# Storing two heads' gK and gV with one DMA of 16 KiB rows in the second pass of an attention backward kernel

## The chip, the cores and the metric

The kernel runs on one core of one Trainium2 chip. The metric is device time in microseconds (us), lower is better: 890.82 us is the median of 3 runs of the kernel before (889.17 to 891.23). A core has five engines with instruction streams of their own: PE (TensorE, matmul), DVE (VectorE), ACT (ScalarE), POOL (GpSimd) and SP (SyncE, which here only issues DMAs). An engine takes its instructions in order; an instruction that waits holds up all behind it. 16 DMA engines move data between HBM and the on-chip memory of 128 partitions.

## The reference

Forward and backward of one decode step: layer norm, attention against a cache, and an MLP, each with a residual, for B=2 sequences, H=32 heads, 4096 cached positions, head size 128, model width 640. What the change touches is the gradient of the cache:

```python
q = (ln(x) @ wq)                        # [2, 32, 1, 128]
p = softmax(q @ k.T * Dh**-0.5)         # k, v: [2, 32, 4096, 128]
h = x + (p @ v) @ wo
h2 = h + relu(ln(h) @ w1) @ w2
# outputs: h2, gx, gK (out_2), gV (out_3), gwq, gwo, gw1, gw2
```

With go the gradient of a head's attention output, gV of a head is the outer product of p and go, and gK is the outer product of gs = p * (v @ go - dot) and the scaled q. Each is 4096 x 128 in bf16, 1 MiB, and there are 64 heads (32 for each sequence).

## The kernel before, in words

**Tiles.** One head's K, V, gK or gV is a tile of 128 partitions x 32 rows x 128 columns: partition p holds cache rows 32p to 32p+31, so a transfer of one tile moves one contiguous row of 8 KiB for each partition (`natural`, L500). 13 such tiles ("homes", `NBIG`) lie in the pool `big`; more come from `big1` (2, where the first pass's pool `pkp` was), from `big2` (1) and from the six tiles of wo when they are no longer needed. `take`, `give` and `share` pass homes between four uses: ld (loads), g (gradients to be stored), f (weight gradients to be stored, called ot) and q (wq and MLP weights).

**Two passes.** The first pass (`p1_iter`, iteration i) loads K and V of each of the 64 heads and makes scores, softmax and the attention output. The second pass (`p2_iter`, iteration j, in the order of the list `turns`) loads V again as Wt, but for 6 kept heads of each sequence, and makes gV and gK. From i=40 on, every second iteration of the first pass has one of the second pass mixed in. When the first pass ends, j=14 to 63 are left: **the second pass alone**, the subject here. Beside it run in small steps (`bg_step`) the MLP's backward, `go_group` (32 reductions at L711 over wo, one for each head of the second sequence), `fin_gen` (weight gradients: PE at L1093, an ACT copy at L1099, a store issued by POOL at L1101) and `gx_gen` (wq loaded once more, 40 reductions at L711).

**One head of the second pass** (`p2_iter`): four groups of four PE transposes of Wt (t_ps, L482), each copied out of PSUM by ACT (t_sb, L487) and multiplied with go by PE (dp, L495); two matmuls that broadcast go and q to all partitions (L985), scaled by ACT into rb (L990); p doubled by POOL (pp, L992); one DVE instruction for gs (L965). Then `outer_half` (L954) makes half of a gradient tile in one DVE instruction: 2 for gK of the head before, 2 for gV of this head. Up to j=32 ACT makes 8 of the 32 row blocks of gV (L1024). SP stores each tile: gK at L1004, gV at L1025. The load of a later head is issued by `pump` as soon as a home is free in the order of the program; it waits on SP for the last transposes of the tile that it overwrites. All of SP's DMAs go through one queue in the order of the program.

**Buffers of this stage before:** ld=10 (6 of them hold kept V, 4 are ahead), g=5; from j=37 on ld=4, g=7 and three tiles of wo, f=3, q=2 and three tiles of wo; once the background is done, still more for g.

Of the kernel before, what the change touches and what calls it, by code (L numbers as in the profile page):

```python
# [7 lines left out]
FP32 = mybir.dt.float32  # L8
BF16 = mybir.dt.bfloat16
ALU = mybir.AluOpType  # L10
# [5 lines left out]
def kernel(  # L16
# [89 lines left out]
    owned = dict(free)  # L106
    wanted = {}
    pools = [big] * NBIG
    home_of = {}
    given_at = {}  # L110

    def take(tag, shape, name):
        assert free[tag] > 0, (tag, name)
        free[tag] -= 1
        k = homes[tag].pop(0)
        t = pools[k].tile(shape, BF16, tag=tag_of.get(k, f"big{k}"), bufs=1, name=name)
        home_of[id(t)] = (tag, k, t)
        return t

    def goes_to(tag):  # L120

        if owned[tag] > wanted.get(tag, len(pools)):
            for other in homes:
                if owned[other] < wanted.get(other, 0):
                    return other
        return tag

    def give(t, to=None):
        tag, k, _ = home_of.pop(id(t))
        to = to or goes_to(tag)  # L130
        owned[tag] -= 1
        owned[to] += 1
        free[to] += 1
        homes[to].append(k)
        given_at[k] = step[0]
# [14 lines left out]
                    d[tag] -= 1  # L150
                    d[to] += 1

    tag_of = {}

    def more_home(tag, pool, name=None):
        if name:
            tag_of[len(pools)] = name
        homes[tag].append(len(pools))
        pools.append(pool)
        free[tag] += 1  # L160
        owned[tag] += 1
# [70 lines left out]
    NPS = 52  # L232
    P_bf = cols.tile([128, NPS, NSC], BF16)
    P_free = list(range(NPS))
    P_slot = {}
    ga = cols.tile([128, B, NF], FP32)
    nc.vector.memset(ga[:], 0.0)
# [127 lines left out]
    qc = pkp.tile([128, H, B], BF16)  # L365
    WH = 6
    NWO = -(-H // WH)
    wo_t = [wop.tile([128, NSC * 128], BF16, tag=f"wo{t}", bufs=1, name="wo_t") for t in range(NWO)]

    def wo_of(h, c0, c1):  # L370
        return wo_t[h // WH][:, (h % WH) * D + c0:(h % WH) * D + c1]
# [73 lines left out]
    pairs = [(b, h) for b in range(B) for h in range(H)]  # L445
    NP1 = len(pairs)
    KEPT = (6, 6)
    GROUPS = []
    for b in range(B):
        first = H - KEPT[b]  # L450
# [497 lines left out]
    def pairs_view(t):  # L948
        return t.rearrange("p s (a two) -> p s a two", two=2)

    def outer_half(dst, row, colp, k, short=0):
        n = HALF - short
        sl = slice(k * HALF, k * HALF + n)
        nc.vector.tensor_tensor(  # L954
            out=pairs_view(dst[:, sl, :]),
            in0=row.rearrange("p (a two) -> p a two", two=2)[:, None, :, :].to_broadcast([128, n, 64, 2]),
            in1=colp[:, sl, None, :].to_broadcast([128, n, 64, 2]), op=ALU.mult)
# [10 lines left out]
        P_free.append(P_slot.pop((bp, hp)))  # L968
        return gsp

    def p2_iter(j, busy, act=0, store=None):
        store = store or nc.gpsimd

        c = S2[j] if j < NP1 else None
        p = S2.get(j - 1)
        if p is not None:
            bp, hp = turns[j - 1]
            gsp = p2_gs(j - 1)
        if c is not None:
            b, h = turns[j]  # L980
            go = gom[:, h, b, :, :]

            bank = pst([128, 512], FP32, "sps", "dp_ps")
            for k, col in enumerate((goc, qsc)):
                nc.tensor.matmul(bank[:, 128 + k * 128:256 + k * 128],  # L985
                                 lhsT=col[:, h, b:b + 1].to_broadcast([128, 128]), rhs=ident_bf[:],
                                 start=True, stop=True)
            c["dp"] = bank[:, 0:NSC]
            rb = mats.tile([128, 256], BF16, tag="rb", bufs=3, name="rb")
            nc.scalar.activation(out=rb[:], in_=bank[:, 128:384], func=ACT.Copy, scale=rt[:, b, h:h + 1])  # L990
            pp = small.tile([128, NSC, 2], BF16, tag="pp", bufs=2, name="pp")
            nc.gpsimd.tensor_copy(out=pp[:], in_=P_bf[:, P_slot[(b, h)], :, None].to_broadcast([128, NSC, 2]))  # L992
            c.update(rb=rb, pp=pp)
            if act:
                pa = small.tile([128, act], FP32, tag="pa", bufs=2, name="pa")
                nc.gpsimd.tensor_copy(out=pa[:], in_=P_bf[:, P_slot[(b, h)], NSC - act:NSC])
            c["T0"] = pair_transpose(c["W"], 0, busy=busy)
        if p is not None:
            gK = take("g", [128, NSC, 128], "gK")
            outer_half(gK, p["rb"][:, 128:256], gsp, 0)  # L1000
        yield
        if p is not None:
            outer_half(gK, p["rb"][:, 128:256], gsp, 1)
            store.dma_start(out=natural(out_2, bp, hp), in_=gK[:])  # L1004
            give(gK)
            del S2[j - 1]
        yield
        if c is None:
            return
        c["T1"] = pair_transpose(c["W"], 1, busy=busy)  # L1010
        pair_matvec(c["dp"], c.pop("T0"), 0, go)
        yield
        c["T2"] = pair_transpose(c["W"], 2, busy=busy)
        pair_matvec(c["dp"], c.pop("T1"), 1, go)
        yield
        c["T3"] = pair_transpose(c["W"], 3, busy=busy)
        give(c["W"], "g" if j < H and j != 1 and owned["g"] < 3 else None)
        pair_matvec(c["dp"], c.pop("T2"), 2, go)
        gV = take("g", [128, NSC, 128], "gV")
        outer_half(gV, c["rb"][:, 0:128], c["pp"], 0)  # L1020
        yield
        outer_half(gV, c["rb"][:, 0:128], c["pp"], 1, act)
        for k in range(act):
            nc.scalar.activation(out=gV[:, NSC - act + k, :], in_=c["rb"][:, 0:128], func=ACT.Copy, scale=pa[:, k:k + 1])  # L1024
        store.dma_start(out=natural(out_3, b, h), in_=gV[:])  # L1025
        give(gV)
        yield


    def p2_tail(j):  # L1030

        p = S2[j]
        bp, hp = turns[j]
        gsp = p2_gs(j)
        yield
        gK = take("g", [128, NSC, 128], "gK")
        outer_half(gK, p["rb"][:, 128:256], gsp, 0)
        yield
        outer_half(gK, p["rb"][:, 128:256], gsp, 1)
        nc.gpsimd.dma_start(out=natural(out_2, bp, hp), in_=gK[:])  # L1040
        give(gK)
        del S2[j]
        yield
# [254 lines left out]
    def p2_step():  # L1298
        nonlocal g2
        try:  # L1300
            next(g2)
        except StopIteration:
            g2 = None

    for n, (i, j) in enumerate(plan):
        all_go = all(("go", B - 1, h) in done for h in range(H))
        if i is None and plan[n - 1][0] is not None:
            pkp.release()
            big1 = tc.alloc_tile_pool(name="big1", bufs=1)
            for _ in range(2):  # L1310
                more_home("ld", big1)
            share(ld=KEPT[1] + 4, g=5)
        if ("w1", B - 1) in done:
            for t in range(NWO):
                if t not in late and all(("go", B - 1, h) in done for h in range(t * WH, min(H, (t + 1) * WH))) and \
                        (t < NWO - 1 or all_go):
                    late[t] = ("g", "g", "g", "q", "q", "q")[len(late)]
                    more_home(late[t], wop, f"wo{t}")
        lq, ll, lg = [sum(v == tag for v in late.values()) for tag in ("q", "ld", "g")]
        if fin is not None and not bg2 and not bg3:  # L1320
            share(ld=4, g=12 + 6 * (lq > 0))
        elif fin is not None and j >= H + KEPT[1] - 1:
            share(ld=4 + ll, g=7 + lg, f=3, q=2 + lq)
        if j is not None:
            while g2 is not None:
                p2_step()
            if j < NP1:
                bg_until(("go", *turns[j]))
            if i is not None and n + 1 < len(plan) and plan[n + 1][1] is None:
                g2 = p2_whole(j)  # L1330
            else:
                g2 = p2_iter(j, 0, 8 if i is None and j <= H else 0, nc.sync if i is None else None)
        if i is None and ("w1", 1) in done and fin is None:
            wts.release()
            fin = tc.alloc_tile_pool(name="fin", bufs=1)
            big2 = tc.alloc_tile_pool(name="big2", bufs=1)
            more_home("f", big2)
            banks.update(sps=[2, 3], o=[4, 5, 6])
            bg2.append(("fin", fin_gen(fin)))
            bg3.append(("gx", gx_gen(fin)))  # L1340
        if i == 12:
# [9 lines left out]
        if i is None:  # L1351
            mixed[0] = False
            spread[0] = 2
            at_k[0] = 1
            k = 0
            while g2 is not None:
                p2_step()
                pump()
                slot[0] = int(k in ((1, 3, 5) if j <= H else (1, 4)))
                k += 1  # L1360
                bg_step(0, rate)
                bg_step(1, RATE2 * (0.4 if spreading[0] else 1.0))
                bg_step(2, RATE3)
            continue
# [64 lines left out]
```

## Time and profile before

| | |
|---|---|
| median of 3 runs | 890.82 us |
| the profiled execution | 887.9 us |
| its span, first to last instruction | 886.1 us (1.8 us lie around it) |
| PE, DVE, ACT, POOL busy | 736.0, 690.8, 478.0, 155.8 us |
| moved by DMA | 361.87 MB, mean 408 GB/s |
| SP's queue | 317.04 MB in 49096 packets |
| first store that SP issues (gK of head 13, the stage alone begins) | issued at 466.7 us |
| last gK store (head 63) | issued at 866.1 us |

A span is cut into windows in the views by stage; for each, the busy time of every engine, the clock granted to PE (1 is full), the share of time in which the 16 DMA engines had packets, and GB/s. A DMA share of 1.01 means that packets overlap by a little and no engine is without one. "Landing" is the time from an issue to the last of the 16 engines' completion marks.

### The profile page before, as it was taken

What the parts mean: (1) busy time and instruction counts of PE and PEld (TensorE: products, weight loads), DVE (VectorE), ACT (ScalarE), POOL (GpSimd) and SP (SyncE); (2) the same over time, 40 slices, a digit from 0 to 9 for tenths busy, and PEclk for the clock granted to TensorE, in tenths of its full rate; (3) what the DMA queues carried; (4) which work ended last, traced back from release to release, by engine and by line L of the source; (5) the groups of instructions that cost most, each with busy time, mean ns of one, the idle gap of its engine ahead of it and who ended that gap; (6) DMA issues with size and microseconds to landing.
All of it is one profiled execution on the core that took longest, in us unless ns stands there. A gap on an engine that the chain in (4) does not pass through costs nothing.

```text
span 886.1 us, 24945 instructions
## 1 busy us (share of the span) xinstructions
PE 736.0 (83%) x10215; PEld 614.3 (69%) x10215; DVE 690.8 (78%) x1309; ACT 478.0 (54%) x1241; POOL 155.8 (18%) x264
## 2 busy tenths in 40 slices
PE   4999899999999998878967777878878896937971
PEld 4888788888888887777856666656757665625640
DVE  2666698877888887777868797678989998799750
ACT  1344343344565655455546777767756555526661
POOL 1344344343210000010011110011010001101200
PEclk9999899999999999999996556555666756556565
DMA  9999999999889999999999999999999999999995
GB/s 377 425 417 417 421 413 420 424 423 416 323 298 392 424 424 426 423 424 426 423 405 415 422 425 425 425 422 412 419 425 414 419 419 427 415 426 421 408 425 229
DMA packets 56115, 361.87 MB, mean 408 GB/s; under 512 B 5712, under 2 KB 11728, under 8 KB 15296
## 3 DMA queue, kind: packets, MB, share of 16 engines
q1 hardware_dynamic: 49096, 317.04, 86.5%
q0 software_dynamic: 6864, 43.22, 11.7%
q8 instruction: 80, 1.31, 0.5%
q14 instruction: 35, 0.29, 0.1%
q10 hardware_dynamic: 40, 0.01, 0.0%
HBM read 211.11 MB, written 149.13 MB: 407 GB/s over the span
## 4 chain that ended last, share of the span: by engine, by line
PE 38%; DMA 21%; DVE 19%; issue 12%; ACT 8%; SPq 0%; POOL 0%; ACTq 0%; POOLq 0%; DVEq 0%
PE t_ps L482 17%; DMA Vt<-in_A_v_cache_dram 10%; PE m_ps L516 9%; DVE gK L954 5%; DVE gV L954 5%; DMA out_dram<-gK 4%; DVE rows L711 4%; DVE pk L523 3%; ACT t_sb L487 3%; PE s_ps L495 3%; PE u_ps L545 3%; DMA out_dram<-ot 2%; ACT gV L1024 2%; DMA wqs<-in_A_wq_dram 2%; PE dp_ps L495 2%
## 5 line engine op out<-in xcount | busy, mean ns | idle before, releaser
L487 ACT COPY t_sb<-t_ps 128x512 f32<-128x512 f32 x479 | 274.2, 587 | 208.7 <-PE t_ps L482 205.4
L495 PEld LDWEIGHTS <-t_sb 128*128 128x128 bf16 x4096 | 177.7, 102 | 57.2 <-ACT t_sb L487 28.8
L482 PE MATMUL t_ps<-ident_f,Wt 128*128 128x128 f32 x832 | 192.6, 381 | 9.0 <-DMA Wt<-in_A_v_cache_dram 8.4
L523 DVE TENSOR_TENSOR pk<-Kt,ep 128x2048 bf16<-128x2048 bf16 x128 | 156.3, 1222 | 39.7 <-ACT ep L570 31.4
L516 PE MATMUL m_ps<-pk,Vt 128*128 128x129 bf16 x2048 | 170.6, 222 | 13.5 <-DMA Vt<-in_A_v_cache_dram 13.5
L482 PEld LDWEIGHTS t_ps<-ident_f,Wt 128*128 128x128 f32 x832 | 134.7, 197 | 38.1 <-issue 30.6
L482 PE MATMUL t_ps<-ident_f,Kt 128*128 128x128 f32 x1024 | 157.0, 286 | 4.1 <-DMA Kt<-in_A_k_cache_dram 3.4
L954 DVE TENSOR_TENSOR gK<-rb,gsp 128x2048 bf16<-128x2048 bf16 x128 | 153.2, 1222 | 8.9 <-DMA out_dram<-gV 7.1
L516 PEld LDWEIGHTS <-Vt 128*128 128x128 bf16 x2048 | 124.5, 98 | 43.5 <-issue 27.7
L954 DVE TENSOR_TENSOR gV<-rb,pp 128x2048 bf16<-128x2048 bf16 (+1 forms) x128 | 143.3, 1140 | 2.7 <-DMA out_dram<-gK 2.6
L482 PEld LDWEIGHTS t_ps<-ident_f,Kt 128*128 128x128 f32 x1024 | 113.5, 145 | 7.8 <-ACT t_sb L487 3.8
L533 POOL COPY pk<-ep 128x16 bf16<-128x16 bf16 x78 | 83.2, 1069 | 155.6 <-ACT ep L570 80.5
L495 PE MATMUL dp_ps<-gom,t_sb 128*128 128x2 bf16 x2048 | 95.3, 168 | 16.9 <-ACT t_sb L487 16.0
L495 PE MATMUL s_ps<-qm,t_sb 128*128 128x2 bf16 x2048 | 87.6, 164 | 1.3 <-DVE t_sb L485 1.3
L1099 ACT CAST ot<-o_ps 128x512 bf16<-128x512 f32 (+3 forms) x152 | 66.8, 493 | 5.1 <-DMA out_dram<-ot 3.0
L992 POOL COPY pp<-P_bf 128x64 bf16<-128x64 bf16 x64 | 30.3, 478 | 163.6 <-DVE gV L954 152.0
L630 ACT CAST wo_t<-m_ps 128x128 bf16<-128x128 f32 x55 | 14.6, 266 | 78.1 <-PE m_ps L516 77.9
L711 DVE CUSTOM_DVE_ANT_0 rows<-wqs,gqr 128x1024 bf16<-128x1024 bf16 x40 | 48.9, 1221 | 9.6 <-DMA wqs<-in_A_wq_dram 9.4
L990 ACT ACTIVATE rb<-dp_ps,rt 128x256 bf16<-128x256 f32 x64 | 30.3, 473 | 44.2 <-PE dp_ps L985 43.3
L711 DVE CUSTOM_DVE_ANT_0 rows<-wo_t,rows 128x640 bf16<-128x640 bf16 x64 | 52.4, 819 | 0.8 <-ACT rows L688 0.4
L1024 ACT ACTIVATE gV<-rb,pa 128x128 bf16<-128x128 bf16 x152 | 46.5, 392 | 6.4 <-DMA out_dram<-gV 6.4
L711 DVE CUSTOM_DVE_ANT_0 rows<-w_t,rows 128x640 bf16<-128x640 bf16 (+2 forms) x53 | 42.3, 799 | 2.9 <-ACT rows L688 2.7
(205 smaller groups left out, 690.3 us busy)
## 6 DMA issues: line engine op xcount, KB each, us to landing
Kt<-in_A_k_cache_dram SPq DMA_DIRECT2D x64, 1024.0 KB, 18.7
Vt<-in_A_v_cache_dram SPq DMA_DIRECT2D x64, 1024.0 KB, 15.1
Wt<-in_A_v_cache_dram SPq DMA_DIRECT2D x52, 1024.0 KB, 16.4
out_dram<-gK SPq DMA_DIRECT2D x51, 1024.0 KB, 16.7
out_dram<-gV SPq DMA_DIRECT2D x50, 1024.0 KB, 15.1
out_dram<-gV POOLq DMA_DIRECT2D x14, 1024.0 KB, 10.4
out_dram<-gK POOLq DMA_DIRECT2D x13, 1024.0 KB, 10.3
out_dram<-ot POOLq DMA_DIRECT2D x6, 960.0 KB, 10.0
```

What stands on the lines that cost most here:

```text
L482: nc.tensor.transpose(t_ps[:, j, :], natf[:, 2 * cc:2 * cc + 2, :].rearrange("p c k -> p (c k)"), ident_f[:])
L487: nc.scalar.copy(out=t_sb[:], in_=t_ps[:])
L495: nc.tensor.matmul(dst[:, sc:sc + 2], lhsT=v[:, j, :, par], rhs=vecs[:, par, :], start=(par == 0), stop=(par == 1))
L516: nc.tensor.matmul(r["m"][:, 0:129], lhsT=r["V"][:, sc, :], rhs=r["pk"][sc // HALF][:, sc % HALF, 0:129], start=(sc == 0), stop=(sc == NSC ...
L523: nc.vector.tensor_tensor(out=p["pk"][k][:, :, 0:128].rearrange("p s (a two) -> p s a two", two=2), in0=p["K"][:, sl, :].rearrange("p s (a ...
L533: nc.gpsimd.tensor_copy(out=col, in_=e)
L711: nc.vector.tensor_tensor_reduce(out=junk[0:kc, 0:width], in0=in0, in1=in1, scale=1.0, scalar=0.0, op0=ALU.mult, op1=ALU.add, accum_out=acc)
L954: nc.vector.tensor_tensor(out=pairs_view(dst[:, sl, :]), in0=row.rearrange("p (a two) -> p a two", two=2)[:, None, :, :].to_broadcast([128 ...
L990: nc.scalar.activation(out=rb[:], in_=bank[:, 128:384], func=ACT.Copy, scale=rt[:, b, h:h + 1])
L992: nc.gpsimd.tensor_copy(out=pp[:], in_=P_bf[:, P_slot[(b, h)], :, None].to_broadcast([128, NSC, 2]))
L1024: nc.scalar.activation(out=gV[:, NSC - act + k, :], in_=c["rb"][:, 0:128], func=ACT.Copy, scale=pa[:, k:k + 1])
L1099: nc.scalar.copy(out=ot[0:kp, k, n0:n0 + nn], in_=o_ps[0:kp, 0:nn])
```

## The change

The stage alone is rewritten to work on two neighbouring heads h and h+1 (h even) of one sequence. Their gK, or gV, lie in one place of 128 partitions x 64 rows x 128 columns: partitions 0 to 63 hold head h, partitions 64 to 127 head h+1, and each partition 64 consecutive cache rows, 16 KiB (`natural2`). One DMA of 2 MiB stores it. V is still loaded head by head with 8 KiB rows, and transposed as before.

- There are two such places at first: `big1`, and homes 3 and 4 of `big` taken together (`TWINS`, `join`/`park`) as soon as both are given up. The third is made of wo's tiles 2 and 3 when the second sequence's heads of both are done with. The list `twos` hands them out in rotation, to gK and gV alternately.
- The other 11 homes of `big` are all for loads: 6 kept and 5 ahead (4 before). From j=37 on ld=7, f=3 and one tile of wo, q=2 and three tiles of wo.
- dp is still made for each head; `halves` then moves the two heads' columns onto 64 partitions each with four small matmuls against `sel`, once for p and once for gs. pp and its fp32 form pa are then copied out of PSUM by ACT, not by POOL; gs is one DVE instruction for each head and one copy for both. rb is made once for the two heads, from four matmuls of 64 columns.
- A period of `p2_two` has as many steps as two of `p2_iter`: the first six make dp of the first head and, between them, gK of the two heads before (`last_gk`, four `outer_half`); then gV's place is taken, dp of the second head is made and gV filled: up to j=32 by 16 ACT instructions, 8 ahead of the second head's four t_sb copies and 8 behind them, and three `outer_half`; after that by four `outer_half`.
- The last gK is stored in two parts of 1 MiB. `short`, `act` and `tag_of` go from the old functions; pp becomes a fixed tile of two parts.

The core of the diff:

```diff
+    big_t = big.tile([128, NBIG, NSC * 128], BF16, name="big_t")
+    place = {k: big_t[:, k, :] for k in range(NBIG)}
...
+    TWINS = (3,)
...
+    def halves(dst, cols_of):
+        for c in range(2):
+            for par in range(2):
+                nc.tensor.matmul(dst[64 * c:64 * c + 64, par * NSC:(par + 1) * NSC], lhsT=sel[:, par, :],
+                                 rhs=cols_of[c], start=True, stop=True)
+
+    def natural2(cache, b, h):
+        return cache[b, h:h + 2].rearrange("h (p sc) d -> (h p) sc d", sc=2 * NSC)
...
+    def last_gk(split=False):
+        p = last[0]
+        gs_of(p["j"] + 1)
+        yield
+        t = S2[p["j"] + 1]["bank"][:, 128:128 + 2 * NSC]
+        halves(t, [ALONE["gs"][:, c, :] for c in range(2)])
+        gsp = pp_t[:].rearrange("p a s two -> p (a s) two")
+        nc.vector.tensor_copy(out=gsp, in_=t[:, :, None].to_broadcast([128, 2 * NSC, 2]))
+        del S2[p["j"]], S2[p["j"] + 1]
+        yield
+        gK = twos.pop(0)
+        out = natural2(out_2, p["b"], p["h"])
+        for k in range(4):
+            outer_half(gK, p["rb"][:, 128:256], gsp, k)
+            if split and k % 2:
+                sl = slice((k - 1) * HALF, (k + 1) * HALF)
+                nc.sync.dma_start(out=out[:, sl, :], in_=gK[:, sl, :])
+            if k < 3:
+                yield
+        if not split:
+            nc.sync.dma_start(out=out, in_=gK[:])
+        twos.append(gK)
+        yield
...
+    def p2_two(j, act):
...
+        def head(k):
...
+            c["T0"] = pair_transpose(c["W"], 0)
+            yield
+            yield
+            c["T1"] = pair_transpose(c["W"], 1)
+            pair_matvec(c["dp"], c.pop("T0"), 0, go)
+            yield
...
+            c["T3"] = pair_transpose(c["W"], 3)
+            give(c["W"])
+            pair_matvec(c["dp"], c.pop("T2"), 2, go)
+            yield
+            yield
...
+        nc.scalar.copy(out=pp[:], in_=bank[:, 384:384 + 2 * NSC, None].to_broadcast([128, 2 * NSC, 2]))
+        if act:
+            nc.scalar.copy(out=pa[:], in_=bank[:, 384 + 2 * NSC - act:384 + 2 * NSC])
+        gV = []
+        def by_act(x0, x1):
+            for x in range(x0, x1 if act else x0):
+                nc.scalar.activation(out=gV[0][:, 2 * NSC - act + x, :], in_=rb[:, 0:128], func=ACT.Copy,
+                                     scale=pa[:, x:x + 1])
+        yield
+        for _ in range(5):
+            next(before, None)
+            next(first)
+            yield
...
+        gV.append(twos.pop(0))
+        by_act(0, act // 2)
+        yield
+        gs_of(j)
+        second = head(1)
+        next(second)
+        yield
+        for k in range(4):
+            next(second)
+            if k < 3 or not act:
+                outer_half(gV[0], rb[:, 0:128], pp, k)
+            yield
+        by_act(act // 2, act)
+        yield
+        next(second)
+        nc.sync.dma_start(out=natural2(out_3, b, h), in_=gV[0])
+        twos.append(gV[0])
+        last[0] = me
...
-            for _ in range(2):
-                more_home("ld", big1)
-            share(ld=KEPT[1] + 4, g=5)
+            twos.append(big1.tile([128, 2 * NSC, 128], BF16, name="two_t"))
...
-                    late[t] = ("g", "g", "g", "q", "q", "q")[len(late)]
-                    more_home(late[t], wop, f"wo{t}")
...
+                    late[t] = "f" if t == NWO - 1 else "q" if t not in (2, 3) else "g"
+                    if late[t] != "g":
+                        more_home(late[t], wop, wo_t[t])
+                    elif sum(v == "g" for v in late.values()) == 2:
+                        twos.append(wo_all[:, 2:4, :].rearrange("p a (s d) -> p (a s) d", d=128))
...
-            share(ld=4 + ll, g=7 + lg, f=3, q=2 + lq)
+            share(ld=7, f=3 + lf, q=2 + lq)
...
+                g2 = p2_two(j, HALF if j <= H else 0)
+            elif i is None:
+                g2 = last_gk(True)
```

## The prediction, made before the changed kernel was run

> **What bounds the kernel now.** I read the page first, then the stage alone (453 to 866 us) in windows, then its DMAs, then one head in order of time. The page's slices and the windows show DMA:
>
> ```profile
> DMA  9999999999889999999999999999999999999995
> 500.00:532.00 32.00, 23.90 (x245) 20.98 (x244) 30.04 (x58) 23.90 (x64) 5.26 (x9) 0.50 1.01 425
> 532.00:560.00 28.00, 19.07 (x210) 16.73 (x209) 22.74 (x38) 21.12 (x60) 2.87 (x7) 0.62 1.01 425
> 700.00:760.00 60.00, 49.73 (x462) 37.34 (x461) 55.77 (x78) 34.04 (x80) 6.23 (x10) 0.56 1.01 422
> 760.00:820.00 60.00, 40.81 (x359) 28.88 (x358) 53.42 (x78) 29.13 (x68) 6.27 (x9) 0.56 1.01 421
> ```
>
> After the window's length stand PE, weight loads, DVE, ACT and POOL, then granted clock, DMA share and GB/s. The DMA share is 1.01 all through the stage at 414 to 425 GB/s, so the 16 DMA engines set the pace. DVE is close behind only late (55.77 of 60). A pair of heads moves 2 loads and 4 stores, 6 tiles of 1 MiB = 6.29 MB; at 425 GB/s that is **14.8 us a pair**. The chain of waits names Vt, gK, t_ps and others in small shares, because it hops between engines that all wait for buffers; I don't price by it.
>
> How full the DMA queue is kept comes next. The loads at the start show the rate of one full queue, and the five tiles of wq, the first transfers of all, what a lone one takes:
>
> ```profile
> 8.27 0.33 SPq L503 DMA_DIRECT2D Kt<-in_A_k_cache_dram  x1
> 10.71 0.33 SPq L503 DMA_DIRECT2D Vt<-in_A_v_cache_dram  x1
> 13.17 0.33 SPq L503 DMA_DIRECT2D Kt<-in_A_k_cache_dram  x1
> DMA to landing us min/median/max: 5.0/7.1/12.7
> ```
>
> SP gets one 1 MiB load off every 2.45 us when the queue is full. The first wq tile, with nothing ahead of it, lands after 5.0 us (the minimum): 2.45 of transfer and **2.6 us that are fixed**. In the stage alone a store lands 12 us (median) after its issue: some 10 us of other work lie ahead of it. Five gradient homes of 1 MiB keep it so: while one is filled, four may be queued.
>
> **The change, part by part.**
>
> *Rows of 16 KiB.* The trace's packet records have a median of 309 ns for 8192 bytes and 159 ns for 4096, and follow one another 306 and 156 ns apart: 6 ns a packet do not scale with size. Each DMA engine carries 8 partitions, so a 2 MiB store is 8 packets of 16 KiB in place of 16 of 8 KiB. 25 gV and 24 gK stores have the long rows: 49 x 8 x 6 ns = **2.4 us less**. Bounds: nothing, if such a row is cut in two again; 49 x 8 x 9 ns + 50 completion packets of 9 ns = 4.0 us if the whole intercept of the durations counts. The only 16 KiB packets of the trace, the 80 of instruction fetch on another queue, last 943 ns, and 392 x (943 - 612) ns would be +130 us; I exclude it because they go to another destination, while 1280 to 8192 bytes of tiles lie on one line. I take 2.4, from the nearest sizes. The Trainium skill, DMA: Bandwidth & Descriptors, section Why small descriptors are slow (HBM only), has 3 cycles of the DMA bus beside each packet's 32-byte beats; an estimate with its 850 MHz makes 304.7 ns of 8 KiB (306 here) and the gain 1.4 us. By it the sum below would be 1.0 us higher.
>
> *Two places of 2 MiB.* gK and gV now take turns with two places, so gV nearly always gets the place that gV had a pair earlier. That place must go round once a period: store, landing, filling, store. Store to landing with an empty queue: 2.6 + 2 x 2.45 = **7.5 us**. Filling, up to j=32, runs through ACT:
>
> ```profile
> 520.00 1.05 ACT L487 COPY t_sb<-t_ps 128x512 f32<-128x512 f32 x2
> 522.05 0.58 ACT L487 COPY t_sb<-t_ps 128x512 f32<-128x512 f32 x1 [0.99 <-PE t_ps L482]
> 523.19 0.58 ACT L487 COPY t_sb<-t_ps 128x512 f32<-128x512 f32 x1 [0.56 <-PE t_ps L482]
> 523.67 2.45 ACT L1024 ACTIVATE gV<-rb,pa 128x128 bf16<-128x128 bf16 x8
> ```
>
> This is one head before: from its first t_sb copy to the end of its 8 ACT rows 6.1 us (520.00 to 526.12), in which ACT waits for PE's transposes. In the changed order 8 more ACT rows, 2.45 us, stand ahead of these four copies and cannot start until the place has landed; behind them on ACT wait the copies, behind these PE's third and fourth group, the release of Wt and the next load. Filling: 2.45 + 6.1 = **8.6 us**; DVE's share (gs 0.28, three halves of 1.22) fits within. The round is 7.5 + 8.6 = **16.1 us** against 14.8: DMA runs dry for 1.3 us a pair. The load of the second head (issued 3 us ahead of the store) does not add: it is through by then. Ten pairs (j=14 to 32): **+13 us**. In the last three, ACT copies of ot fall into the filling (25 of 0.4 us between 566 and 625 us, half of them: +1.5 a round), but ot's own transfers (2 of 1 MB, +1.6 us a pair of DMA work) then fill the gap; I cost both at nothing. Bounds: 0.3 to 2.4 us a pair (below, and for the round's jitter, which nothing queued absorbs), +3 to +24. By the Trainium skill, same page, section Anatomy of one DMA, a transfer issued by GpSimd takes 2.0 us + bytes / 436 GB/s; that would make 6.8 us of the 7.5, the round 15.4 and this term 6; the wq tile's 5.0 us (4.4 by the formula) speaks for mine.
>
> *Pairs 34 and 36*, still with two places (the 20th reduction over wo, which frees tiles 2 and 3, runs at 620 us): gV by DVE, 0.28 + 4 x 1.22 + two reductions of 0.9 = 7.0; round 14.5, no loss. gK's round: four halves and some reductions, 7 us, the same.
>
> *The start.* Before, the first gV leaves at 471.35, when W loads and gK of head 13 are queued to 476.6. Now the first gV leaves a whole pair's work later, some 11 us (482.5); only two loads (2.45 each, released by heads 14 and 15) come between, a third if a g home has become one for loads. DMA idles 0 to 5 us: **+1.5**.
>
> *Three places* (j from 38): a place comes back after 1.5 periods, at 16.7 us a pair 25 us; filling is at most half a period, 8.4, plus 7.5 of landing leaves 9 us of queue: no loss. *The end*: the last gK leaves at 866.09 with 19 us of transfers ahead; 2.4 us more of DVE hide behind them. Loss 0, up to 3.
>
> *Small instructions*: DVE for each pair +0.1 (one PSUM copy, near gs's 0.28; two gs half as wide), PE 8 more matmuls of 32 columns (near 0.1 each), ACT one rb less (0.46) and two small copies more (0.46 at most each), POOL loses pp and pa (0.5 + 0.5 a head), SP 50 issues of 0.33. All hide behind DMA; where the round binds, ACT's copies lie outside it. If that cover went, 0.5 us x 25.
>
> **Sum.** -2.4 + 13 + 1.5 = **+12.1 us**. On the profiled execution's 887.9: 900.0. The median of the runs shown is 2.9 higher: **902.9**.
>
> **Rivals** (all on the median's footing).
>
> *The round is hidden (faster).* The filling hangs on PE's clock: four transposes take 1.10 us at the granted 0.50 of 500 to 532, but 0.60 at full clock (around 455 us). Two such groups lie in the chain, so at full clock it is 7.6 and the round 15.1; and a pair of before, by landings, takes that too (gV of head 17 landed at 502.6, of head 32 at 620.7: 15.75 us a pair, less 0.63 for 2 MB of ot). Up to 15.1 nothing is lost and only the rows count: 890.8 - 2.4 to - 4 = **888**. For it: PE has less to do, and the clock was 0.69 in the first window; against: it fell to 0.50 as the stage went on. Chance 0.28.
>
> *DVE becomes the bound late.* At 700 to 760 DVE has 4.2 of 60 us free, 1.2 us a pair. If coarse places make it wait over that, each further us a pair costs 14: one is **917**. For: 7 loads now stand between stores. Against: loads and stores alternate on SP. Chance 0.12.
>
> *The rows come out in 8 KiB pieces*, the rest as forecast: **905**, within the forecast's own range.
>
> *Loss and gain cancel* (round at 15.1 to 15.3): **891**, chance 0.10.
>
> **Numbers.** Forecast 0.50, its own range 894 to 910. A difference of 0.2% (1.8 us) is about what measuring can tell from no change. Faster is the first rival's, 0.28; same the last one's, 0.10; slower the forecast and the late DVE bound, 0.62. From 885.5 to 914 some 2 in 10 are left out: the rows' best case with a better start below, the late DVE bound above.
>
> **What would show it.** Right: between 470 and 620 us the DMA share falls under 1, GB/s under 400, and ACT's first gV row waits for the landing of gV's store; pairs there are 16 us apart. Stores of 2 MiB with 16 KiB packets of some 609 ns. From 640 us on GB/s at or over 422. Wrong: DMA share 1.01 in the early windows (first rival), or DVE waiting for stores late (second).

## The result and the profile after

| | before | after |
|---|---|---|
| median | 891.03 us (889.17 to 893.5, 4 runs) | **925.52 us** (924.57 to 927.9, 4 runs) |
| profiled span | 886.1 us | 923.3 us |
| granted clock, mean | 0.789 | 0.768 |

The ratio is **1.0389 [1.0357, 1.0422]**: the change costs 34.5 us (the 891.03 counts one run more than the 890.82 ahead). The prediction had 902.9 (885.5 to 914.0): the sign is right, the loss nearly three times as large. Of the runs below, one execution of the last kernel in the table (920.1 us, granted clock 0.654) was slow; without it that kernel's median is 896.67 and not 896.94, and its ratio leaves it out.

The slices of the page and the same four windows as before (length, busy PE, weight loads, DVE, ACT, POOL, granted clock, DMA share, GB/s), after the change:

```profile
DMA  9999999999889999999989999897998999999988
500.00:532.00 32.00, 22.45 (x234) 19.11 (x232) 22.54 (x41) 21.16 (x58) 0.00 (x0) 0.50 0.91 354
532.00:560.00 28.00, 20.31 (x204) 17.32 (x203) 22.43 (x43) 17.46 (x49) 0.00 (x0) 0.50 1.00 387
700.00:760.00 60.00, 52.06 (x561) 41.77 (x560) 52.70 (x81) 32.88 (x76) 1.63 (x3) 0.67 0.94 384
760.00:820.00 60.00, 45.11 (x421) 32.74 (x420) 54.15 (x79) 30.61 (x76) 1.60 (x3) 0.56 1.01 421
```

DMA no longer runs through the stage: 0.91 and 354 GB/s where it was 1.01 and 425. Every engine is less busy as well (DVE 22.54 of 32 us, before 30.04), so no engine has become the bound. From 760 to 820 us the two kernels look alike again.

How much is lost where? Each of the 16 DMA engines leaves a mark when it has done its part of a transfer. I follow gV's store by the first of these 16 marks, before and after:

| odd head j of the pair | 15 | 17 | 23 | 31 | 33 | 35 | 37 | end of span |
|---|---|---|---|---|---|---|---|---|
| before, us | 484.25 | 499.24 | 543.40 | 605.46 | 624.22 | 639.00 | 653.33 | 886.1 |
| after, us | 492.73 | 509.68 | 559.66 | 638.70 | 657.89 | 672.45 | 690.86 | 923.3 |
| later by | 8.5 | 10.4 | 16.3 | 33.2 | 33.7 | 33.5 | 37.5 | 37.2 |

Before, the 16 marks of a store spread over up to 8 us; by their median the last row is 6.9, 9.2, 15.0, 31.2, 32.4, 32.2 and 36.3, the same picture.

The delay of the end has arisen by j=37, while there are two places: some 10 us at the start, of which about 2 come along from the first pass (gK of head 13 is issued at 468.52, before at 466.73); 1.9 a pair in the three quiet pairs to j=23 (16.66 us a pair; before 14.72, the 14.8 of the prediction's count of bytes); 4.2 a pair in the four to j=31, beside which the weight gradients are made; nothing in the next two; 4.1 in the last, that of j=37.

Behind it, with three places, it does not simply stand still: gV's marks of j=39 to 63 are 38 to 51 us later than before, and the end again 37.2. One gap can be named. SP issues no load between 679.23 and 717.15 us, and from 700 to 710 us the DMA share is 0.59 at 247 GB/s, some 4 us of work at 422. So the last pairs lose a little and the end makes it good; neither was taken apart.

What waits, between 455 and 680 us (engine, line, releaser: us in total, times, longest):

```profile
PEld L531 <- ACT t_sb L523: 38.2, 29, 13.2
ACT two_t L1172 <- DMA out_dram<-two_t: 30.5, 7, 12.9
PE dp_ps L531 <- ACT t_sb L523: 30.3, 16, 12.8
DVE two_t L990 <- DMA out_dram<-two_t: 20.9, 6, 10.3
```

The same two kinds in the trace of before, same stretch:

```profile
PEld L495 <- ACT t_sb L487: 25.5, 41, 2.1
ACT gV L1024 <- DMA out_dram<-gV: 6.4, 1, 6.4
```

ACT's first row of gV (L1172) now waits 30.5 us for the landing of the store that held the place, before once, 6.4 us. And PE's waits for t_sb copies, which stand behind that row on ACT, last up to 13.2 us; before, none was over 2.1. A quiet round, in order of time:

```profile
520.14 0.34 SPq L1196 DMA_DIRECT2D out_dram<-two_t  x1
...
527.03 2.45 ACT L1172 ACTIVATE two_t<-rb,pa_t 128x128 bf16<-128x128 bf16 x8 [0.27 <-DMA out_dram<-two_t]
529.38 1.05 ACT L523 COPY t_sb<-t_ps 128x512 f32<-128x512 f32 x2
531.42 0.58 ACT L523 COPY t_sb<-t_ps 128x512 f32<-128x512 f32 x1 [1.00 <-PE t_ps L518]
533.16 0.58 ACT L523 COPY t_sb<-t_ps 128x512 f32<-128x512 f32 x1 [0.57 <-PE t_ps L518]
533.65 2.45 ACT L1172 ACTIVATE two_t<-rb,pa_t 128x128 bf16<-128x128 bf16 x8
536.12 0.34 SPq L1196 DMA_DIRECT2D out_dram<-two_t  x1
```

gV leaves, 6.9 us later the place is free (ACT had waited 0.27 us for it), filling takes 9.1 us, gV leaves: 16.0. And a round that something disturbed, ACT and SP:

```profile
608.34 0.34 SPq L1196 DMA_DIRECT2D out_dram<-two_t  x1
...
621.05 2.44 ACT L1172 ACTIVATE two_t<-rb,pa_t 128x128 bf16<-128x128 bf16 x8 [6.45 <-DMA out_dram<-two_t]
629.28 0.33 SPq L539 DMA_DIRECT2D big_t<-in_A_v_cache_dram  x1
```

Here a store of ot, issued by POOL at 599.8 us, gK's store of 598.5 and a load of 605.3 were all issued ahead of gV's store. The place comes back after 12.7 us, not 6.9, all of ACT's queue stands behind it, and SP gets no load off between 611.9 and 629.3 us. The gK store of 618.5 is the only one issued in between, and gV of that pair leaves 24.1 us after the one before. While ACT waits, DMA is still busy (share 0.97 from 598 to 621 us); behind the wait it runs dry (0.59 from 621 to 634 us, at 234 GB/s).

The three rounds before this one, between the gV stores of 552.87, 572.16, 591.22 and 608.34 us, last 19.3, 19.1 and 17.1 us, and in them the filling grows too. The second, ACT and SP:

```profile
572.16 0.34 SPq L1196 DMA_DIRECT2D out_dram<-two_t  x1
...
578.94 2.44 ACT L1172 ACTIVATE two_t<-rb,pa_t 128x128 bf16<-128x128 bf16 x8
...
584.50 0.58 ACT L523 COPY t_sb<-t_ps 128x512 f32<-128x512 f32 x1 [1.31 <-PE t_ps L518]
584.99 0.59 ACT L1271 CAST ot<-o_ps 128x512 bf16<-128x512 f32 x1
...
591.22 0.34 SPq L1196 DMA_DIRECT2D out_dram<-two_t  x1
```

The place is free after 6.8 us, as in the quiet round, but filling it takes 12.3 us and not 9.1: the copies of ot, and ACT's waits for PE's transposes, stand between the copies of the second head.

### The profile page after: what moved, and what is told of

Same layout as the page of the kernel before. It is cut to its first block, busy times and chain, and to the rows that moved or that the text cites. A ratio compares the mean times of both kernels' runs of the same rounds, so it can differ in the third digit from the quotient of the medians.

```text
span 923.3 us, 24993 instructions
## 1 busy us (share of the span) xinstructions
PE 756.5 (82%) x10415; PEld 632.0 (68%) x10415; DVE 691.3 (75%) x1324; ACT 476.5 (52%) x1259; POOL 123.3 (13%) x197
## 3 DMA queue, kind: packets, MB, share of 16 engines
q0 software_dynamic: 6864, 43.22, 11.4%
## 4 chain that ended last, share of the span: by engine, by line
PE 33%; DMA 29%; issue 17%; DVE 15%; ACT 5%; SPq 0%; POOL 0%; DVEq 0%; ACTq 0%; POOLq 0%
PE t_ps L518 14%; DMA big_t<-in_A_v_cache_dram 12%; PE m_ps L552 8%; DMA out_dram<-wo_t 8%; DMA out_dram<-two_t 4%; DVE big_t L990 4%; DVE pk L559 3%; PE s_ps L531 3%; ACT t_sb L523 2%; DMA out_dram<-big_t 2%; PE u_ps L581 2%; DVE rows L747 2%; DVE wo_t L990 2%; PE o_ps L1265 2%; DMA big_t<-in_A_k_cache_dram 2%
## 5 line engine op out<-in xcount | busy, mean ns | idle before, releaser
L518 PE MATMUL t_ps<-ident_f,big_t 128*128 128x128 f32 x2048 | 398.5, 336 | 6.8 <-DMA big_t<-in_A_k_cache_dram 3.8
L518 PEld LDWEIGHTS t_ps<-ident_f,big_t 128*128 128x128 f32 x2048 | 277.5, 171 | 40.8 <-issue 21.8
L559 DVE TENSOR_TENSOR pk<-big_t,ep 128x2048 bf16<-128x2048 bf16 x128 | 156.3, 1222 | 39.4 <-ACT ep L606 31.1
L552 PE MATMUL m_ps<-pk,big_t 128*128 128x129 bf16 x2048 | 170.2, 222 | 14.4 <-DMA big_t<-in_A_v_cache_dram 14.3
L552 PEld LDWEIGHTS <-big_t 128*128 128x128 bf16 x2048 | 124.0, 98 | 45.2 <-issue 27.6
L990 DVE TENSOR_TENSOR big_t<-rb,pp_t 128x2048 bf16<-128x2048 bf16 x108 | 128.2, 1218 | 10.0 <-DMA out_dram<-big_t 9.8
L531 PE MATMUL dp_ps<-gom,t_sb 128*128 128x2 bf16 x2048 | 96.0, 168 | 33.5 <-ACT t_sb L523 31.1
L990 DVE TENSOR_TENSOR two_t<-rb,pp_t 128x2048 bf16<-128x2048 bf16 x74 | 87.5, 1219 | 23.4 <-DMA out_dram<-two_t 23.3
L1172 ACT ACTIVATE two_t<-rb,pa_t 128x128 bf16<-128x128 bf16 x160 | 48.9, 392 | 30.5 <-DMA out_dram<-two_t 30.5
L747 DVE CUSTOM_DVE_ANT_0 rows<-big_t,wo_t 128x1024 bf16<-128x1024 bf16 x40 | 48.7, 1218 | 0.0
L990 DVE TENSOR_TENSOR wo_t<-rb,pp_t 128x2048 bf16<-128x2048 bf16 x36 | 42.5, 1220 | 3.9 <-DMA out_dram<-wo_t 3.9
L1068 PEld LDWEIGHTS <-sel 128*64 128x64 bf16 x200 | 12.0, 148 | 31.2 <-issue 30.6
## 6 DMA issues: line engine op xcount, KB each, us to landing
big_t<-in_A_v_cache_dram SPq DMA_DIRECT2D x116, 1024.0 KB, 12.3
big_t<-in_A_k_cache_dram SPq DMA_DIRECT2D x64, 1024.0 KB, 19.3
out_dram<-big_t POOLq DMA_DIRECT2D x29, 1024.0 KB, 10.4
big_t<-in_A_wq_dram SPq DMA_DIRECT2D x10, 1024.0 KB, 15.6
```

Of the source, the lines that this page charges most:

```text
L518: nc.tensor.transpose(t_ps[:, j, :], natf[:, 2 * cc:2 * cc + 2, :].rearrange("p c k -> p (c k)"), ident_f[:])
L531: nc.tensor.matmul(dst[:, sc:sc + 2], lhsT=v[:, j, :, par], rhs=vecs[:, par, :], start=(par == 0), stop=(par == 1))
L552: nc.tensor.matmul(r["m"][:, 0:129], lhsT=r["V"][:, sc, :], rhs=r["pk"][sc // HALF][:, sc % HALF, 0:129], start=(sc == 0), stop=(sc == NSC ...
L559: nc.vector.tensor_tensor(out=p["pk"][k][:, :, 0:128].rearrange("p s (a two) -> p s a two", two=2), in0=p["K"][:, sl, :].rearrange("p s (a ...
L747: nc.vector.tensor_tensor_reduce(out=junk[0:kc, 0:width], in0=in0, in1=in1, scale=1.0, scalar=0.0, op0=ALU.mult, op1=ALU.add, accum_out=acc)
L990: nc.vector.tensor_tensor(out=pairs_view(dst[:, sl, :]), in0=row.rearrange("p (a two) -> p a two", two=2)[:, None, :, :].to_broadcast([128 ...
```

## The experiments

All but one are the changed kernel with an edit; none leaves out work. Times are medians; intervals are those of the ratio to the kernel before on the same chip (890.0 to 890.3 us there, 891.0 beside the changed kernel's 925.5, so up to 1 us of the last column may be the chip).

| | us | ratio | against 925.5 |
|---|---|---|---|
| ACT's rows behind the copies | 913.79 | 1.0265 [1.0231, 1.03] | -11.7 |
| third place throughout | 932.32 | 1.0475 [1.0445, 1.0505] | +6.8 |
| home 10 withheld at the start | 921.88 | 1.0368 [1.0326, 1.041] | -3.6 |
| rows of 8 KiB | 930.76 | 1.0448 [1.0409, 1.0487] | +5.2 |
| gV by DVE alone | 907.17 | 1.0202 [1.0158, 1.0245] | -18.4 |
| third place, handed back | 904.07 | 1.0175 [1.0148, 1.0203] | -21.5 |
| the same, ACT's rows behind | 906.95 | 1.02 [1.018, 1.022] | -18.6 |
| places in halves | 913.35 | 1.0273 [1.0248, 1.0299] | -12.2 |
| third place, home 10 | 904.12 | 1.0176 [1.0137, 1.0215] | -21.4 |
| and places at the end | 906.27 | 1.0195 [1.0156, 1.0234] | -19.3 |
| and gV by DVE | 899.08 | 1.0109 [1.0077, 1.0141] | -26.4 |
| before, with four homes for gradients | 892.28 | 1.0037 [1.0009, 1.0065] | |
| halves, third place, home 10, DVE | 896.36 | 1.0063 [1.0038, 1.0088] | -29.2 |
| halves, two places, home 10, DVE | 896.94 | 1.008 [1.0048, 1.0112] | -28.6 |

Two theories stood against each other at first. **P**: the wait for a place is the loss, passed on through ACT. **C**: a pair's chain of PE and ACT, at the granted 0.50, is itself as long as the period, and places don't matter.

**The order of ACT's work.**

```diff
-        by_act(0, act // 2)
         yield
         gs_of(j)
...
-        by_act(act // 2, act)
+        by_act(0, act)
```

> The changed kernel with one move: ACT's first 8 rows of gV stand behind the second head's four t_sb copies, with the other 8, so that nothing of the second head waits on ACT for gV's place. Theory P (a place comes back too late, and the wait stands in front of the second head's work): ACT waited 30.5 us for the places' landings, 17.6 of them after the start; most of these and the stalls behind them go, 10 to 18 us less than the changed kernel's 925.5, so 908 to 915. Theory C (the pair's own chain of PE and ACT takes as long as the period, whatever the places do): the chain has the same instructions, 922 to 928.

Measured 913.79: P's range. Its waits between 455 and 680 us:

```profile
PEld L531 <- ACT t_sb L523: 18.3, 29, 3.8
DVE two_t L990 <- DMA out_dram<-two_t: 19.7, 7, 8.1
ACT two_t L1172 <- DMA out_dram<-two_t: 3.9, 2, 2.0
```

The place is waited for as before, but by DVE (19.7 us, before this edit 20.9), behind which the second head's copies do not stand. ACT's wait falls from 30.5 to 3.9 us and PE's from 38.2 to 18.3. ACT's work is the same, so C alone does not explain 11.7 us. DMA moves 416 GB/s in 500 to 560 us (the changed kernel 369), but only 355 in 560 to 640 (336): the order mends the quiet pairs and not those beside which ot is made.

**A third place throughout.** `TWINS = (3, 10)` joins homes 10 and 11 as well; three loads ahead are left.

> The changed kernel with a third place of 2 MiB from the second pair on (two more homes taken together), and so 3 loads ahead in place of 5. Theory P: a place has 1.5 periods to come back, the rounds fall from 16 to 17.7 us a pair to DMA's 14.8 to 15.1, some 15 to 20 us less over ten pairs: 905 to 911. Theory C: the chain of a pair stays at 15 to 16 us, 2 to 5 us less: 920 to 924. If fewer loads ahead is what hurts, it is slower than 925.

Measured 932.32, slower than the changed kernel and outside both theories. The trace shows two things. Up to head 37 the run does what P says: gV of that pair is issued at 654.2 us (680.0 in the changed kernel). But the last gK is issued at 889.5, and then 40 us follow in which gx's 40 reductions over wq are finished: they start from 745.2 to 855.1 us in the changed kernel, from 809.1 to 923.6 in this one. wq is read into homes of use q, and the joined homes are missing there: wq_t comes only into wo's tiles, the five loads one after the other up to 909.9 us. So the edit moved a shortage, and its time says nothing on P. It had to be done again with the homes handed back.

**The start.** Home 10 becomes a load's home with gK of head 13; the next load takes it and waits on SP for that store's landing at 477.17 us, and two more loads and gV's first store stand behind. In the changed kernel, from the store of gK of head 13 on, SP issues:

```profile
468.52 0.35 SPq L1212 DMA_DIRECT2D out_dram<-big_t  x1
477.32 1.28 SPq L539 DMA_DIRECT2D big_t<-in_A_v_cache_dram  x3
478.70 0.62 SPq L1196 DMA_DIRECT2D out_dram<-two_t  x1
```

For 8.8 us SP issues nothing; then three loads go ahead of gV in one lump, and gV's first mark comes 14.0 us after its issue (492.73). The edit keeps such homes in a list and gives them to the loads only after that store.

```diff
             else:
-                homes["ld"].append(k)
-                free["ld"] += 1
-                owned["ld"] += 1
+                owed.append(k)
```

> The changed kernel, in which the home that head 13's gK was stored from becomes one for loads only after the first gV's store has been issued, so that no load on SP waits for that store's landing (477.2 us) ahead of the first gV. Theory S (the start's 24.7 us between the first two gV stores comes from SP, blocked until 477.3, and from four loads that then run ahead of gV): the first period falls to 16 to 18, 6 to 9 us less, 917 to 920. If the start is a matter of two places alone, within 2 us of 925.5.

Measured 921.88, between the two cases (917 to 920, and within 2 us of 925.5). The first gV's mark comes at 488.1 us, 4.6 us earlier, and the first period is 18.4 us (480.85 to 499.29) where it was 24.7; 3.6 us are left at the end, and the intervals of the two ratios overlap, so its worth is not clear of noise.

**Rows of 8 KiB.** Each 2 MiB store becomes two DMAs of 1 MiB with 8 KiB rows, issued at the same point.

```diff
-        nc.sync.dma_start(out=natural2(out_3, b, h), in_=gV[0])
+        for sl in (slice(0, NSC), slice(NSC, 2 * NSC)):
+            nc.sync.dma_start(out=natural2(out_3, b, h)[:, sl, :], in_=gV[0][:, sl, :])
```

> The changed kernel with each 2 MiB store issued as two DMAs of 1 MiB with 8 KiB rows, both at the point where the one stood. By the packet records a 16 KiB packet takes 611 ns and two of 8 KiB 618: 49 x 8 x 7 ns = 2.7 us more where DMA is the bound, less where it idles: 926 to 929. If long rows were themselves the loss, it would be faster than 925 by more than 2.

Measured 930.76, just above the range; the intervals overlap a little. By this the long rows gain about 5 us, in a kernel where a store's landing is waited for: ACT's wait for places is 42.6 us here and 30.5 with them.

```profile
ACT two_t L1173 <- DMA out_dram<-two_t: 42.6, 9, 12.0
```

**gV by DVE alone.** `p2_two(j, 0)` in place of `p2_two(j, HALF if j <= H else 0)`.

> gV is filled by VectorE alone (four outer_half, 4.9 us), ScalarE's 16 row blocks (2 x 2.45 us a pair, ten pairs) are gone. Theory P (what a pair loses is the wait for its place, and it is paid because ScalarE's rows stand ahead of the t_sb copies that TensorE needs): VectorE waits for the place, TensorE runs on; 906 to 914, as with the rows behind the copies (913.8). Theory S (ScalarE's own time in the pair's chain is the loss): more than that order gave, 900 to 907. Rival D (VectorE becomes the bound with one more outer_half a pair): 918 to 926.

Measured 907.17, in P's range and at the edge of S's, so it does not tell the two apart. DVE's extra half a pair costs nothing that shows; rival D falls. The places are still two, whole, and waited for (DVE 24.1 us), but DMA moves 408 GB/s in 500 to 560 us and 398 in 560 to 640.

**The third place, handed back** when wo's place comes:

```diff
-    TWINS = (3,)
+    TWINS = (3, 10)
...
+                        ap = twin[TWINS[1]][2]
+                        twos[:] = [t for t in twos if t is not ap]
+                        for k in (TWINS[1], TWINS[1] + 1):
+                            del twin[k]
+                            homes["ld"].append(k)
```

> A third place from the second pair on, out of two load homes, given back to the loads as soon as wo's place exists; otherwise as the changed kernel. Theory P: the two-place stage costs nothing more, gV of head 37 is issued near 654 us as in the run with three places throughout (680 in the changed kernel), and what follows lasts as long as in the changed kernel: 897 to 905. Theory C (a pair's chain of TensorE and ScalarE at the half clock sets the pace, places do not matter; three places throughout gained nothing in the end): 918 to 928. In between, 905 to 915: part of what is gained is given back because only three loads are ahead.

**With ACT's rows behind the copies as well:**

> As the run with the third place handed back, and ScalarE's 16 rows all behind the second head's copies. Theory P: with no wait for a place left, the order of ScalarE's work is worth little: within 4 us of that run, 895 to 903. Theory C: the order is worth its 11.7 us here too: 886 to 894, or 10 to 12 below that run wherever it lies.

Measured 904.07 and 906.95. The first is in P's range; the second is within 4 us of it, as P asks, though above the 895 to 903 reckoned from that. With three places the order of ACT's work is worth nothing that can be told, though it was worth 11.7 us with two. C falls as the cause of the whole loss. The windows 500 to 560 and 560 to 640 us of the changed kernel, then with the third place:

```profile
500.00:560.00 60.00, 42.76 (x436) 36.43 (x434) 44.96 (x83) 38.62 (x106) 0.00 (x0) 0.50 0.95 369
560.00:640.00 80.00, 55.11 (x521) 43.83 (x520) 49.73 (x100) 50.98 (x147) 1.06 (x2) 0.52 0.87 336
```

```profile
500.00:560.00 60.00, 42.41 (x460) 37.02 (x459) 49.37 (x90) 44.49 (x125) 0.00 (x0) 0.59 1.00 409
560.00:640.00 80.00, 65.27 (x656) 51.97 (x655) 62.25 (x129) 57.03 (x162) 2.15 (x4) 0.56 0.98 394
```

From 336 to 394 GB/s in the second window, and all engines do more work in it. Some 14 us of the loss are left.

**Places in halves.** Two places as in the changed kernel, but each half of a gK or gV is stored when its two `outer_half` are done, as 1 MiB with 8 KiB rows.

```diff
             if k < 3 or not act:
                 outer_half(gV[0], rb[:, 0:128], pp, k)
+            if k == 1:
+                nc.sync.dma_start(out=natural2(out_3, b, h)[:, 0:NSC, :], in_=gV[0][:, 0:NSC, :])
```

> Each 2 MiB place is stored as two 1 MiB halves, each as soon as its two outer_half are done, with 8 KiB rows. To compare with 930.8 us, the same two pieces at one point. Theory P (two places held too long: the whole place waits for its whole store): the first half leaves 2 to 4 us earlier and is free earlier, so a round shortens by 2 to 4 us: 916 to 926. If the grain of the store does not matter: 928 to 932.

Measured 913.35, under P's range: 17.4 us less than with the same pieces issued at one point (930.76), so the moment at which a place's parts leave matters. Against the changed kernel it is 12.2 us, and its windows are still far from full (374 GB/s in 500 to 560 us, 359 in 560 to 640): with ACT's rows where they are, halves alone do not do it.

**What is left: start, end, ACT.** Three kernels, each with one edit more on the third place.

> The third place handed back (904.1 us alone) and home 10 withheld from the loads until the first gV is stored (3.6 us alone). If the start is a loss of its own: 899 to 902. If the third place already covers it (gV's first place no longer has to wait there): 903 to 906.

> As the run before, and homes that no load uses any more become places once no load is left to issue (up to four homes, two places). If the last pairs wait for their places: 3 to 6 us less than that run, about 896 to 898. If TensorE and VectorE at the half clock set the last pairs: within 1 us of it.

> As the run before, and gV by VectorE alone. Theory P (with a place always free ScalarE's rows cost next to nothing, as their order did): within 3 us of that run. Theory S (ScalarE's 4.9 us a pair are in the pair's chain): 6 to 10 us less, 887 to 893.

Measured 904.12, 906.27 and 899.08. Withholding home 10 adds nothing to the third place, as in the second of its cases. More places at the end bring nothing (2.2 us more, with intervals that overlap), so nothing shows that the last pairs wait for places. Taking ACT's rows away is worth 7.2 us against the run before it and 5.0 against the one before that, where the intervals still touch: nearer to theory S than to P's 3, though the 887 to 893 is missed, since it was reckoned from an end that gained. So a part of ACT's 4.9 us a pair, 0.5 to 0.7 us, stands in the pair's chain of PE and ACT even with a third place; that much of C holds.

**The kernel before with four homes for gradients**: `share(ld=KEPT[1] + 5, g=4)` for `share(ld=KEPT[1] + 4, g=5)`. This is the changed kernel's space, in its old pieces.

> The kernel before with four gradient homes and five loads ahead from the start of the second pass alone, in place of five and four: the same buffer space as in the changed kernel, in pieces of 1 MiB of one head. Theory P, space alone decides: 15 to 25 us slower than before. Theory G, what costs is that the space comes in two pieces that are each filled and stored whole: within 5 us of before.

Measured 892.28, some 2 us over before. From 500 to 560 us DMA is as full as before (from 560 to 640 it moves 399 GB/s, before 419):

```profile
500.00:560.00 60.00, 41.10 (x419) 35.72 (x417) 49.59 (x91) 43.52 (x115) 8.89 (x16) 0.54 1.01 425
```

So the space alone is not what costs 34.5 us. Theory G, the two pieces that are each filled and stored whole, is the case left of the two; but this kernel also works head by head in the old order, so the run does not show G by itself.

**The grain, with ACT's rows gone.** Halves, gV by DVE, home 10 withheld: once with the two places of the changed kernel, once with the third.

> Two places as in the changed kernel, in halves stored as soon as ready, gV by VectorE alone and home 10 withheld. Theory G (the grain of a place, not its space, sets the two-place stage): the loss of that stage is gone without a third place: 895 to 902. If two whole places limit it even so: 906 to 912.

> As the run with all of it but the end (third place handed back, home 10 withheld, gV by VectorE alone; with the end's places it was 899.1 us), and each place stored in two halves of 1 MiB as soon as each is ready, with 8 KiB rows. If what is left over the kernel before (9 us) is still the grain of the stores: 889 to 894. If the grain is settled by the third place, the shorter rows cost their 5 us: 901 to 906. If what is left is a compute bound end: 897 to 901.

Measured 896.94 and 896.36. With halves, two places do as well as three. The windows of the run with two places:

```profile
500.00:560.00 60.00, 39.65 (x434) 34.80 (x433) 52.77 (x91) 25.26 (x53) 0.00 (x0) 0.59 1.01 425
560.00:640.00 80.00, 62.03 (x632) 49.66 (x631) 66.35 (x132) 38.94 (x91) 2.16 (x4) 0.59 1.01 408
```

28.6 of the 34.5 us go without any buffer more. They are not the grain's alone: gV by DVE gave 18.4 of them with whole places, and halves and home 10 together the other 10.2. GB/s in the two windows show who mends what:

| | 500 to 560 us | 560 to 640 us |
|---|---|---|
| before | 425 | 419 |
| changed | 369 | 336 |
| ACT's rows behind the copies | 416 | 355 |
| places in halves | 374 | 359 |
| gV by DVE alone | 408 | 398 |
| third place, handed back | 409 | 394 |
| halves, two places, home 10, DVE | 425 | 408 |

So more than half of the loss hangs on ACT's part in filling two whole places: without ACT's rows 18.4 us go, with a third place 21.5. The run with the third place, 896.36, lies 0.6 us under the case of a compute bound end and 2.4 over that of the grain; its interval, 893.7 to 898.2 us, reaches into both, so it rules out only the third case. These last 6 us (8.5 between the profiled spans of 894.6 and 886.1) have no single cause that a run names; the traces say where they are. By (GB/s of before - GB/s) x length / 425, the windows of the two-place run at 450 to 500, 560 to 640 and 640 to 700 us (397, 408 and 397, before 412, 419 and 419) make 1.8 + 2.1 + 3.1 us. And 2 x 5 x 100 / 425 = 2.4 us lie ahead of the changed stage, where the loads of the first pass run slower, in this kernel and in the changed one alike (changed kernel, then before):

```profile
0.00:100.00 100.00, 83.42 (x1373) 73.91 (x1374) 55.81 (x120) 35.52 (x101) 35.00 (x58) 0.98 1.00 406
100.00:200.00 100.00, 97.52 (x1717) 85.19 (x1716) 82.33 (x162) 39.55 (x120) 41.28 (x53) 0.99 1.02 415
```

```profile
0.00:100.00 100.00, 83.77 (x1395) 74.63 (x1396) 55.66 (x120) 35.99 (x102) 35.22 (x58) 0.98 1.00 411
100.00:200.00 100.00, 98.33 (x1727) 86.02 (x1726) 82.91 (x164) 40.22 (x123) 41.39 (x53) 0.99 1.02 420
```

Why is open. No version beat the kernel before; the best are 29 us better than the changed one.

## Why the prediction was right in kind and wrong in size

**Rows of 16 KiB, -2.4: right.** Packets of 16 KiB have a median of 611 ns in the trace, two of 8 KiB 618: 7 ns x 49 x 8 = 2.7 us. The run with 8 KiB rows says about 5, with intervals that overlap; there a landing is waited for as well. The Trainium skill, DMA: Bandwidth & Descriptors, section Why small descriptors are slow (HBM only), by which the gain would be 1.4 us as an estimate, is lower than either; the trace does not bear it out.

**The round of a place, 7.5 + 8.6 = 16.1: right as a sum.** The quiet round is 6.9 + 9.1 = 16.0. The landing was taken too long at 7.5, as the shortest 2 MiB stores land after 6.7 to 6.9 us. The Trainium skill, same page, section Anatomy of one DMA, states its formula for transfers issued by GpSimd; the estimate of 6.8 us from it is nearer than my 7.5 for these stores issued by SP. The quiet pairs lose 1.9 us each and not 1.3: only one of their three rounds is 16.0, the other two are 16.7 us, and in those the place is free 8.2 us after the store (6.8 in the one of 16.0). What made these two landings longer was not taken apart.

**Two places, +13 for ten pairs: the step that failed.** It said of the last pairs that "ACT copies of ot fall into the filling", that "ot's own transfers ... then fill the gap", and "I cost both at nothing". They fill nothing: between the gV stores of 552.87 and 632.45 us POOL issues one store of ot (599.8), and DMA moves 336 GB/s from 560 to 640 us where it moved 419. The four rounds in between last 15.6 us longer than four quiet ones. 9.6 of these lie between gV's store and ACT's first row in the same place (9.6, 6.8, 8.1 and 12.7 us; quiet 6.9), and the one store of ot is among the work issued ahead in the longest. The other 6.0 lie in the filling (9.7, 12.3, 9.0 and 11.4 us; quiet 9.1), where ACT's and PE's work for the weight gradients stands between the copies of the second head. By the marks, the four pairs from j=23 to 31 lost 17.0 us where 5 were allowed; without ACT's rows the same window moves 398 GB/s. From gV of j=15 to that of j=33, nine of the ten rounds, 25.2 us (33.7 - 8.5) are lost, against nine times 1.3. The sum took the round as a fixed number to be compared with DMA's need, but with two places, each filled and stored whole, nothing absorbs a longer landing or a longer filling: every disturbance is added, and none is made good.

**Pairs 34 and 36 at nothing**: right for the first (33.7 to 33.5), 4.1 us off for the second; that was not taken apart.

**The start, +1.5, bounds 0 to 5: wrong.** It is 8.5 to 10.4 us, less the 2 that come along from the first pass. The prediction named the third load and missed that it waits on SP for a landing, with two loads and gV's store behind it; by the run without that wait it is worth 3.6 us, not clear of noise. The rest was not taken apart by itself. With home 10 withheld, halves and gV by DVE together, 450 to 500 us moves 397 GB/s where it was 368 (before 412).

**Three places no loss, the end at nothing: right in sum, in part by luck.** The delay is 37.5 us at j=37 and 37.2 at the end, but some 4 us are lost between 700 and 710 us with three places, and the end makes up for it and more; the prediction has neither.

**Small instructions at nothing: not tested by themselves.** ACT's rows, which the prediction saw only in the filling, cost 5 to 7 us even with a third place.

**The rivals.** The hidden round asked for the full clock; it was 0.50 in 500 to 560 us. A DVE bound late is not seen: from 760 to 866 us DMA is at 1.00 to 1.01, and the end is no later than j=37 was. Rows in 8 KiB pieces: the packets are of 16 KiB. The signs named under "what would show it" came as written, but for the rounds, 16 to 17 us apart in the quiet pairs and 17 to 24 in the four with ot, and for GB/s from 640 us, which is 401 to 700 us and 384 to 760, not 422.

## What to carry to other kernels

A larger store saves a few nanoseconds a packet; the buffer behind it is also filled as one and freed as one, and that is the larger price. When a stage is bound by DMA, count what each buffer's round (store, landing, filling) leaves over against the period: with nothing left over, whatever lengthens the round, a transfer of others in front of the store or other work in the filling, is lost for good, so price the disturbed round and not the quiet one. Where a place may be waited for, put the waiting instruction on an engine, or at a point of its queue, behind which no work of the critical chain stands; and store the parts of a buffer when they are ready.

## What the runs showed of the hardware

A kernel that stalls was not granted more clock here: in the windows from 500 and 560 us it was 0.50 and 0.52 where DMA stood at 369 and 336 GB/s, and 0.59 in both in the run with halves, gV by DVE and home 10 withheld, where 425 and 408 GB/s were moved. Which comes first was not tested. A low clock alone does not make the loss: the kernel before was granted 0.50 from 500 to 532 us and moved 425 GB/s.
